# Experts' products on scaled pairs of 16-bit floats, with the weights prepared in the down blocks

## The chip, the cores and the metric

The kernel runs on one core of one Trainium2 chip. The metric is the device time of one execution in microseconds (us); the time before is the median of three runs. A core has TensorE (matrix products, results in PSUM), VectorE, ScalarE and GpSimd (elementwise work; GpSimd has no way into PSUM), and SyncE, whose queue issues the transfers here. In the rows these are PE (its weight loads PEld), DVE, ACT, POOL and SP. Each engine takes its own instructions in the order in which the program issues them, and engines wait for each other through semaphores that the planner of the tiles sets.

## The reference

Attention with a learned position bias, a layer of three gated products, and a layer of eight experts that are mixed by a normalised matrix:

```python
x = attention(q, k, v, bias)                      # 1152 tokens x 512
h = np.maximum(np.maximum(x @ w1, x @ w2), x @ w3)   # 1152 x 768
x = h @ w_out                                     # 1152 x 512
logits = x @ w_gate                               # 1152 x 8
P = np.exp(logits - logits.max())
for _ in range(8):
    P /= P.sum(1, keepdims=True) + 1e-09
    P /= P.sum(0, keepdims=True) + 1e-09
    P *= N / E
for e in range(8):
    out += P[:, e:e+1] * (np.maximum(x @ w1[e], 0) @ w2[e])   # 512 -> 1024 -> 512
```

All inputs are 32-bit floats; moe_w1 to moe_w3 and w_out reach the chip as 64-bit floats.

## The kernel before

Products that need more than the matrix engine's short format are done on pairs: a number is split into a high part (rounded to the short 32-bit format, F32R) and a low part (what is left), and three products, high by high, high by low and low by high, are summed in PSUM. ScalarE rounds the high part, VectorE or GpSimd subtracts for the low part.

The stages in order of time: the bias table (to 74 us), attention (to some 215 us), the first product of the gated layer (`m1_mm`, to 324 us), its output product (L890 to L900, to 362 us), the experts (from 362 us on).

*First product.* 18 pieces, f in 0 to 5 (128 hidden columns) by g in 0 to 2 (384 tokens). Each has three products of 12 matmuls with 384 columns; ScalarE copies the first (`t1`, L784), VectorE takes the two maxima (L786, L789), ScalarE rounds (L790), and VectorE subtracts for the low part one piece later (the list `lows`, L791). Between them `w_step` hands out the preparation of the next weights in single steps: the seven lambdas of `prep_w64` (L105 to L114) on ScalarE, four times VectorE, ScalarE, GpSimd. The order in the program is the order in each engine's queue.

*Output product.* 16 pieces (d by g) of 18 matmuls with 288 columns. ScalarE copies each into `x2f`. The list `steps` puts the work for the experts between the pieces: `x_split` makes high and low parts of the seven blocks that the scheme below needs (`b_steps`, `x_steps`), and `prep_f(0)` the first expert weights.

*Experts.* Each expert has two halves (256 hidden rows of each of two blocks); a half expert h is two "up" blocks, `up(2h)` and `up(2h+1)`, and one "down" block, `down(h)`. The order of issue is up 0, up 1, up 2, down 0, up 3, up 4, down 1, and so on. An up block does a 2x2 block product with seven products in place of eight, each 12 matmuls of 288 columns (two halves of tokens, two slices of the inner dimension, three pairs), into the PSUM tiles x, y and z (two banks each); ScalarE copies partial products out (`snap`), VectorE adds and subtracts, ScalarE rounds the rectified result (`relu_hi`) and VectorE makes the low part (`relu_lo`). A down block has nine tiles of 128 tokens; each is 12 matmuls of 512 columns into one of two banks (`pd`), added to `acc` on VectorE with the weight P. Down 0 and 1 differ: in down 0 ScalarE copies and VectorE does the steps `rows` and `cols` that normalise P, one of eight after each tile, with a small product on TensorE; in down 1 GpSimd multiplies by P.

The weights of an up block come as four blocks (512 KB, `load_f`); `prep_f` makes four sums on VectorE (`s13`, `s24`), rounds on ScalarE (`a_split`, `hi_s`) and subtracts on GpSimd (`a_split`) and VectorE (`lo_s`). The weights of a down block are four tiles of 256 KB (`load_2`, `prep_2`). Both are handed out between the seven products of the up block before (the dictionary `extra`, by the number of the product). `logits` is done on the split parts of x, between products of up 0 (`between`).

## Time and profile before

| what | value |
|---|---|
| three runs | 1127.1, 1127.91, 1130.8 us; median 1127.91 |
| profiled execution | span 1128.2 us (its time is given by its span alone) |
| TensorE busy | 1093.3 us (97%) |
| VectorE, ScalarE, GpSimd busy | 692.3, 497.7, 366.5 us |
| mean granted clock of TensorE | 0.992 |

A profile is one execution. Busy time is the union of an engine's instructions; matmuls overlap in it, so a group's mean is longer than the distance from one matmul to the next. The chain of waits is followed back from the last instruction: at each step to what released it.

### The profile page before, as it was taken

How to read it: one execution, taken by the hardware profiler on the slowest of the kernel's cores; microseconds unless marked ns; L12 is line 12 of the kernel's file. 1: busy time of each engine (PE TensorE's matmuls, PEld its weight loads, DVE VectorE, ACT ScalarE, POOL GpSimd, SP SyncE). 2: the span in 40 equal slices, each digit the busy share in tenths (PEclk: the TensorE clock that was granted, in tenths of full speed). 3: DMA queues.
4: the chain of work that ended last, by engine and by line, in shares of the span. 5: the costliest groups of instructions: out<-in, count | busy, mean ns of one | idle time of the engine just before them, and what ended most of it. 6: DMA issues, size and time to landing. Idle time of an engine off the chain costs nothing.

```text
span 1128.2 us, 18182 instructions
## 1 busy us (share of the span) xinstructions
PE 1093.3 (97%) x7162; PEld 985.8 (87%) x7162; DVE 692.3 (61%) x1214; ACT 497.7 (44%) x903; POOL 366.5 (32%) x258
## 2 busy tenths in 40 slices
...
GB/s 186 266 243 253 217 188 109 40 114 113 109 20 39 76 19 48 28 75 15 62 47 29 76 11 65 48 28 75 13 63 47 28 76 14 62 48 28 57 19 85
DMA packets 36148, 88.49 MB, mean 78 GB/s; under 512 B 5535, under 2 KB 6494, under 8 KB 35166
## 3 DMA queue, kind: packets, MB, share of 16 engines
...
## 4 chain that ended last, share of the span: by engine, by line
PE 76%; DVE 13%; issue 3%; ACT 3%; POOL 2%; DMA 2%; DVEq 0%; SPq 0%; ACTq 0%; POOLq 0%
PE d L1092 35%; PE x L1010 12%; PE y L1010 9%; PE z L1010 8%; PE o L895 3%; PE sc L469 2%; POOL s L343 2%; PE pv L607 2%; DVE ww L106 2%; PE pt L555 1%; DVE ww L111 1%; PE m L658 1%; DVE ng L486 1%; DVE ww L109 1%; PE p L368 1%
## 5 line engine op out<-in xcount | busy, mean ns | idle before, releaser
L1078 POOL TENSOR_TENSOR w2l<-w2r,w2h 128x512 fp32r<-128x512 f32 x64 | 93.6, 1463 | 477.7 <-ACT w2h L1077 469.4
L1106 DVE SCALAR_TENSOR_TENSOR acc<-d,P,acc 128x512 f32<-128x512 f32 x126 | 94.6, 751 | 224.0 <-PE d L1092 223.9
L1092 PE MATMUL d<-w2h,hh 128*128 128x512 f32 x576 | 224.9, 390 | 0.0
L1092 PE MATMUL d<-w2h,hl 128*128 128x512 f32 x576 | 224.6, 390 | 0.0
L1092 PE MATMUL d<-w2l,hh 128*128 128x512 f32 x576 | 224.4, 390 | 0.0
L1018 ACT ACTIVATE s<-x 128x576 f32<-128x576 f32 x96 | 62.5, 651 | 352.8 <-PE x L1010 349.4
L1023 ACT ACTIVATE hh<-s 128x576 fp32r<-128x576 f32 x128 | 87.9, 687 | 93.6 <-DVE s L1035 44.6
L1092 PEld LDWEIGHTS d<-w2h,hl 128*128 128x128 f32 x576 | 108.1, 188 | 23.0 <-DVE hl L1028 0.3
L1092 PEld LDWEIGHTS d<-w2l,hh 128*128 128x128 f32 x576 | 108.2, 188 | 22.0
L1092 PEld LDWEIGHTS d<-w2h,hh 128*128 128x128 f32 x576 | 108.2, 188 | 21.8
L1028 DVE SCALAR_TENSOR_TENSOR hl<-s,hh 128x576 fp32r<-128x576 f32 x128 | 102.1, 815 | 1.8 <-ACT hh L1023 1.5
L835 POOL TENSOR_TENSOR w1l<-wf,w1h 128x768 fp32r<-128x768 f32 x32 | 59.8, 1870 | 77.5 <-ACT w1h L834 67.5
L1010 PE MATMUL x<-xth,w1h 128*128 128x288 f32 x384 | 82.4, 296 | 0.5 <-ACT acc L898 0.5
L1010 PE MATMUL x<-xtl,w1h 128*128 128x288 f32 x384 | 82.2, 296 | 0.0
L1010 PE MATMUL x<-xth,w1l 128*128 128x288 f32 x384 | 82.1, 295 | 0.0
L658 PE MATMUL m<-xh,wh 128*128 128x384 f32 x216 | 73.2, 339 | 2.0 <-DVE t L786 1.9
L658 PE MATMUL m<-xh,wl 128*128 128x384 f32 x216 | 72.8, 337 | 0.7 <-POOL wl L114 0.7
L658 PE MATMUL m<-xl,wh 128*128 128x384 f32 x216 | 72.6, 336 | 0.0
L1044 DVE TENSOR_TENSOR s<-y,s 128x576 f32<-128x576 f32 x32 | 24.2, 757 | 70.4 <-ACT w1h L838 59.4
L1010 PEld LDWEIGHTS x<-xth,w1h 128*128 128x128 f32 x384 | 62.5, 189 | 1.8 <-ACT acc L898 0.7
L1010 PEld LDWEIGHTS x<-xtl,w1h 128*128 128x128 f32 x384 | 61.8, 189 | 0.0
L1010 PEld LDWEIGHTS x<-xth,w1l 128*128 128x128 f32 x384 | 61.8, 189 | 0.0
...
## 6 DMA issues: line engine op xcount, KB each, us to landing
...
w2r<-in_moe_w SPq DMA_DIRECT2D x64, 256.0 KB, 2.6
...
```

What stands on the lines that cost most here:

```text
L106: lambda: V.tensor_scalar(out=f, in0=f, scalar1=2.0 ** -15, scalar2=None, op0=ALU.max),
L658: T.matmul(out=p[:, :TG], lhsT=ws[:, 128 * c:128 * c + 128], rhs=xs[:, c, TG * g:TG * g + TG], start=(c == 0 and n == 0), stop=(c == 3 and ...
L835: G.tensor_tensor(out=lo[:, 0:3], in0=t[:, 1:4], in1=raw(hi[:, 0:3]), op=ALU.subtract)
L895: T.matmul(out=p[:, :SH], lhsT=ws[:, 128 * d:128 * d + 128], rhs=xs[:, f, SH * g:SH * g + SH], start=(k == 0), stop=(k == 17))
L1010: T.matmul(out=ps[bank][:, s, :SH], lhsT=ws[:, i, c, :], rhs=xs[:, j, c, s * SH:s * SH + SH], start=(start and k == 0), stop=(k == 5), **kw)
L1018: A.activation(out=t, in_=src, func=AF.Copy)
L1023: A.activation(out=o, in_=src, func=AF.Relu)
L1028: V.scalar_tensor_tensor(out=l, in0=src, scalar=0.0, in1=raw(o), op0=ALU.max, op1=ALU.subtract)
L1044: V.tensor_tensor(out=s2, in0=y, in1=s2, op=ALU.add)
L1078: G.tensor_tensor(out=lo, in0=r, in1=raw(hi), op=ALU.subtract)
L1092: T.matmul(out=pd, lhsT=hs[:, fh, 128 * t:128 * t + 128], rhs=ws, start=(k == 0), stop=(k == 11))
L1106: V.scalar_tensor_tensor(out=acc[:, t, :], in0=pd, scalar=P[:, t, e:e + 1], in1=acc[:, t, :], op0=ALU.mult, op1=ALU.add)
```

## The change

The operands of the experts' products become pairs of 16-bit floats (F16) in place of pairs in F32R. To keep the numbers in the range of that format, they are multiplied by powers of two: x by one common factor, each half expert's two weight matrices by a factor each, the hidden result by one common factor, and the sum in `acc` is multiplied back (`gains`, `kh`).

- The factors come from largest absolute values. VectorE takes maxima (`peak`): over each piece of the first product's result and over the output weights, over each piece of `x2f`, and over each weight matrix of the experts (`peak_w`). The maxima of the partitions are brought together on TensorE for x and the hidden result (`x_top`, `x_scale`, `m_top`, `m_spread`), and for the expert weights by a transfer to DRAM and one back to all partitions (`peak_send`, `peak_get`), after which VectorE takes the maximum and makes the powers (`peak_all`, `powers`).
- ScalarE multiplies while it copies (a scale per partition): `snap`, the copy of `x2f`, and two new operations, `scale` for a set of up weights and one per tile of down weights, in place.
- The subtraction in `lo_s` goes from VectorE to GpSimd. Adding and subtracting a product in an up block becomes a multiply-add (`join`).
- The preparation of all weights of the experts goes from the up blocks into the down block of the half expert before (the dictionary `todo`, by tile), apart from the first ones. The raw weights are loaded further ahead (four sets of up weights, eight tiles of down weights), and the split down weights have two buffers (`w2s`).
- `logits` uses `x2f` and the gate weights as full 32-bit floats: 16 products with the outputs in four column groups, in place of 40 on split parts.
- In up 0 the first copy is issued after the second product.

```diff
+    peak = [] if top_to is None else [
+        lambda: V.tensor_reduce(out=top_to, in_=f, op=ALU.max, axis=AX.XY, apply_absolute_value=True)]
...
+def powers(out, m):
+
+    i = out.bitcast(I32)
+    n = m.shape[-1]
+    V.tensor_scalar(out=m, in0=m, scalar1=TINY, scalar2=None, op0=ALU.max)
+    V.tensor_scalar(out=i[:, 0:n], in0=m.bitcast(I32), scalar1=EXPM, scalar2=EXPM,
+                    op0=ALU.bitwise_and, op1=ALU.bitwise_xor)
+    V.tensor_scalar(out=i[:, n:2 * n], in0=m.bitcast(I32), scalar1=EXPM, scalar2=None, op0=ALU.bitwise_and)
...
+def peak_out(n, m):
+    w = m.shape[-1]
+    peaks_d[n] = dram.tile([128 * w], F32, name="peaks" + "".join(map(str, n)))
+    dma(peaks_d[n].rearrange("(p w) -> p w", w=w), m)
...
+        w = src.shape[0]
+        peaks_s[n] = scl.tile([128, 256], F32, tag="all", name="all", bufs=2)[:, 0:w]
+        dma(peaks_s[n], src.unsqueeze(0).to_broadcast([128, w]))
...
+def peak_in(n, out):
+    peak_get(n)
+    V.tensor_reduce(out=out, in_=peaks_s.pop(n).rearrange("p (k w) -> p w k", k=128), op=ALU.max, axis=AX.X)
+
+def peak(out, in_):
+    V.tensor_reduce(out=out, in_=in_, op=ALU.max, axis=AX.X, apply_absolute_value=True)
+
+def load_f(n):
+    if n < NE * 4:
+        w1r[n] = (w1e if n % 4 < 2 else w_pool[2]).tile([128, 4, 2, 128], F32, tag="wr1", name="wr1", bufs=2)
+        dma(w1r[n], a["moe2_w1"][n // 4, n % 4])
...
+def peak_all(name, items):
+
+    items = [x for x in items if x[0] < 2 * NE]
+    if items:
+        m = scl.tile([128, 2], F32, tag="pm", name="pm", bufs=2)[:, 0:len(items)]
+        peak_in(name, m)
+        for i, (h, kind) in enumerate(items):
+            o = scl.tile([128, 4], F32, tag=f"pw{kind}", name="pw", bufs=4)
+            powers(o, m[:, i:i + 1])
+            V.tensor_scalar(out=o[:, 2:3], in0=o[:, 0:1], scalar1=2.0 ** (11 if kind == 1 else 13),
+                            scalar2=None, op0=ALU.mult)
+            w_pow[h, kind] = o
...
-        w_pool[:] = mp, 6
+        w_pool[:] = mp, 6, None
+        for n in range(2):
+            load_f(n)
+        S10 = ("a",), [(0, 1)]
+        SB = ("b",), [(1, 1), (0, 2)]
+        SC = ("c",), [(1, 2)]
+        w_early = {(2, 0): lambda: peak_w(0, 1, 0), (2, 2): lambda: [peak_w(0, 1, 1), peak_join(*S10)],
+                   (3, 2): lambda: peak_send(S10[0]), (4, 1): lambda: peak_get(S10[0]),
+                   (5, 1): lambda: peak_all(*S10)}
...
-                lows.append(lambda t2=t2, o=o, l=hl[:, f, TG * g:TG * g + TG]: V.tensor_tensor(
-                    out=l, in0=t2, in1=raw(o), op=ALU.subtract))
+
+                def low(t2=t2, o=o, l=hl[:, f, TG * g:TG * g + TG], m=mo[0][:, 3 * f + g:3 * f + g + 1]):
+                    V.tensor_tensor(out=l, in0=t2, in1=raw(o), op=ALU.subtract)
+                    peak(m, t2)
+
+                lows.append(low)
+                w_early.get((f, g), lambda: None)()
                 w_step(4)
...
-    xth = xtp.tile([128, 7, 2, S], F32R, name="xth")
-    xtl = xtp.tile([128, 7, 2, S], F32R, name="xtl")
...
+    xth = xtp.tile([128, 7, 2, S], F16, name="xth")
+    xtl = xtp.tile([128, 7, 2, S], F16, name="xtl")
...
             return []
-        t = w1f_t.pop(n)
-        hi = w1s.tile([128, 7, 2, 128], F32R, tag="w1h", name="w1h")
-        lo = w1s.tile([128, 7, 2, 128], F32R, tag="w1l", name="w1l")
+        t = w1s.tile([128, 8, 2, 128], F32, tag="wf", name="wf", bufs=1)
+        hi = w1s.tile([128, 7, 2, 128], F16, tag="w1h", name="w1h")
+        lo = w1s.tile([128, 7, 2, 128], F16, tag="w1l", name="w1l")
         w1s_t[n] = hi, lo
+
+        def scale():
+            A.activation(out=t[:, 0:4], in_=w1r.pop(n), func=AF.Identity, scale=w_pow[n // 2, 1][:, 2:3])
+            load_f(n + 4)
...
             A.activation(out=hi[:, 0:3], in_=t[:, 1:4], func=AF.Copy)
-            G.tensor_tensor(out=lo[:, 0:3], in0=t[:, 1:4], in1=raw(hi[:, 0:3]), op=ALU.subtract)
+            G.tensor_tensor(out=lo[:, 0:3], in0=t[:, 1:4], in1=hi[:, 0:3], op=ALU.subtract)
...
         def lo_s():
-            V.tensor_tensor(out=lo[:, 3:7], in0=t[:, 4:8], in1=raw(hi[:, 3:7]), op=ALU.subtract)
-            load_f(n + 1)
-
-        return [s13, s24, a_split, hi_s, lo_s]
+            G.tensor_tensor(out=lo[:, 3:7], in0=t[:, 4:8], in1=hi[:, 3:7], op=ALU.subtract)
+
+        return [scale, s13, s24, a_split, hi_s, lo_s]
...
+    def x_top():
+        pm = ps_s.tile([128, 2, 512], F32, tag="sc", name="pmh")
+        T.transpose(pm[:2, 0, :128], mho, ident)
+        V.tensor_reduce(out=nho, in_=pm[:2, 0, :128], op=ALU.max, axis=AX.X)
+        V.tensor_scalar(out=dho, in0=ident[0:2, 0:2], scalar1=nho, scalar2=None, op0=ALU.mult)
...
+    def x_scale():
+        pm = ps_s.tile([128, 2, 512], F32, tag="sc", name="pmh2")
+        T.matmul(out=pm[:, 0, 0:2], lhsT=ones[0:2, :], rhs=dho, start=True, stop=True)
+        V.tensor_copy(out=mho, in_=pm[:, 0, 0:2])
+        powers(pho, mho)
+        for i in range(2):
+            V.tensor_scalar(out=xs[:, i:i + 1], in0=pho[:, 2 * i:2 * i + 1], scalar1=pho[:, 2 * i + 1:2 * i + 2],
+                            scalar2=0.5, op0=ALU.mult, op1=ALU.mult)
...
+    bs0, bs1, xs0, pf0, last = b_steps(0), b_steps(1), x_steps(0), prep_f(0), []
+    pf1 = prep_f(1)
+    sched = {0: [x_top], 1: [x_scale], 2: [pf0[0]], 3: [pf0[1], pk(1, 1, 0)], 4: [pf0[2], pk(1, 1, 1), bs0[0]],
+             5: [pf0[3], pk(0, 2, 0), bs0[1]], 6: [pf0[4], pk(0, 2, 1), pk(0, 2, 2)],
+             7: [pk(0, 2, 3), lambda: peak_join(*SB), pf0[5]],
+             8: xs0[0:2], 9: xs0[2:4], 10: xs0[4:5] + pf1[0:1] + [lambda: peak_send(SB[0])], 11: pf1[1:3],
+             12: bs1[0:1] + pf1[3:4], 13: bs1[1:2] + pf1[4:5] + [lambda: peak_get(SB[0])],
+             14: [lambda: last[0]()], 15: [lambda: last[1](), pf1[5]]}
...
+            def x_ev(k=k, p=p, o=x2f[:, d, SH * g:SH * g + SH]):
+                A.activation(out=o, in_=p[:, :SH], func=AF.Identity, scale=xs[:, 0:1])
+                peak(xm[:, k:k + 1], o)
+
+            evs.append(x_ev)
+            if k < 2:
+                sched[k][0]()
+            if k > 0:
+                while evs:
+                    evs.pop(0)()
+            if k == 15:
+                V.tensor_reduce(out=m2[:, 0:1], in_=xm, op=ALU.max, axis=AX.X)
+            for step in sched.get(k, ())[k < 2:]:
                 step()
...

-    def logits(b):
-
-        blocks = ((0, 0), (1, 1)) if b == 0 else ((0, 0), (0, 3), (1, 2))
-        for n in range(2):
-            p = ps_d.tile([128, 512], F32, tag="d", name="pl")
-            mm = [(ws, xs[:, blk, c, n * SH:n * SH + SH], 2 * dh + c)
-                  for dh, blk in blocks for c in range(2) for ws, xs in zip(wgs, (xth, xtl))]
-            for k, (ws, xs, c) in enumerate(mm):
-                T.matmul(out=p[0:2 * NE, :SH], lhsT=ws[:, c, :], rhs=xs, start=(k == 0), stop=(k == len(mm) - 1))
-            A.activation(out=lt[:, b * S + n * SH:b * S + n * SH + SH], in_=p[0:2 * NE, :SH], func=AF.Copy)
+    def logits():
+
+        p = ps_d.tile([128, 512], F32, tag="d", name="pl")
+        for k in range(4):
+            for c in range(4):
+                T.matmul(out=p[32 * c:32 * c + NE, :SH], lhsT=wg[:, k, :], rhs=x2f[:, k, SH * c:SH * c + SH],
+                         start=(k == 0), stop=(k == 3))
+        for c in range(4):
+            A.activation(out=lt[:, SH * c:SH * c + SH], in_=p[32 * c:32 * c + NE, :SH], func=AF.Identity,
+                         scale=xs[0:NE, 1:2])
...
+    def m_top():
+        pm = ps_d.tile([128, 512], F32, tag="d", name="pmx")
+        T.transpose(pm[:1, :128], m2[:, 0:1], ident)
+        V.tensor_reduce(out=nm2, in_=pm[:1, :128], op=ALU.max, axis=AX.X)
+
+    def m_spread():
+        pm2 = ps_d.tile([128, 512], F32, tag="d", name="pmx2")
+        T.matmul(out=pm2[:, 0:1], lhsT=ones[:1, :], rhs=nm2, start=True, stop=True)
+        V.tensor_copy(out=m2[:, 1:2], in_=pm2[:, 0:1])
+        powers(cx[:, 0:2], m2[:, 1:2])
+        V.tensor_scalar(out=c, in0=cx[:, 0:1], scalar1=2.0 ** -9, scalar2=None, op0=ALU.mult)
+        V.tensor_scalar(out=nc_, in0=c, scalar1=-1.0, scalar2=None, op0=ALU.mult)
+        V.tensor_scalar(out=kx, in0=cx[:, 1:2], scalar1=xs[:, 1:2], scalar2=2.0 ** 8, op0=ALU.mult, op1=ALU.mult)
+
+    between = {(0, 0): [m_top, last[2]], (0, 1): [m_spread, last[3]], (0, 3): [last[4], logits], (1, 0): [flip], (1, 1): [gate],
+               (0, 4): [lambda: peak_all(*SB)], (0, 6): [pk(1, 2, 0), pk(1, 2, 1)], (1, 5): [],
+               (1, 2): [pk(1, 2, 2), pk(1, 2, 3), lambda: peak_join(*SC)],
+               (1, 4): [lambda: peak_send(SC[0])], (2, 2): [lambda: peak_get(SC[0])], (2, 5): [lambda: peak_all(*SC)]}
...
+    def gains(h):
+        kh = kh_t[h] = sk.tile([128, 1 + NTT], F32, tag="kh", name="kh", bufs=2)
+        o1, o2 = w_pow[h, 1], w_pow[h, 2]
+        V.tensor_scalar(out=kh[:, 0:1], in0=o1[:, 1:2], scalar1=o2[:, 1:2], scalar2=kx, op0=ALU.mult, op1=ALU.mult)
+        V.tensor_scalar(out=kh[:, 0:1], in0=kh[:, 0:1], scalar1=2.0 ** -26, scalar2=None, op0=ALU.mult)
+        if h > 1:
+            V.tensor_scalar(out=kh[:, 1:], in0=P[:, :, h // 2], scalar1=kh[:, 0:1], scalar2=None, op0=ALU.mult)
...
-        hhi = h_p.tile([128, 2, NT], F32R, tag="hh", name="hh")
-        hlo = h_p.tile([128, 2, NT], F32R, tag="hl", name="hl")
+        hhi = h_p.tile([128, 2, NT], F16, tag="hh", name="hh")
+        hlo = h_p.tile([128, 2, NT], F16, tag="hl", name="hl")
...
-            A.activation(out=t, in_=src, func=AF.Copy)
+            A.activation(out=t, in_=src, func=AF.Identity, scale=c)
             return t
+
+        def join(out, z, scale):
+            V.scalar_tensor_tensor(out=out, in0=z, scalar=scale, in1=out, op0=ALU.mult, op1=ALU.add)
...
-        s1 = snap("s1", prod(A11, B11, "x", True))
+        x = prod(A11, B11, "x", True)
+        if n > 0:
+            s1 = snap("s1", x)
         then(0)
         z = prod(A12, B21, "z", True)
-        V.tensor_tensor(out=s1, in0=z, in1=s1, op=ALU.add)
+        if n == 0:
+            then(1)
+            s1 = snap("s1", x)
+        join(s1, z, c)
         relu_hi(0, 0, s1)
-        then(1)
+        if n > 0:
...
         y = prod(S4, B22, "y", False)
-        V.tensor_tensor(out=s2, in0=y, in1=s2, op=ALU.add)
...
-        V.tensor_tensor(out=s3, in0=s3, in1=z, op=ALU.subtract)
+        join(s3, z, nc_)
...
             c, fh = i // 2 % 2, i % 2
-            hi = w2p.tile([128, DM], F32R, tag=f"w2h{c}{fh}", name="w2h")
-            lo = w2p.tile([128, DM], F32R, tag=f"w2l{c}{fh}", name="w2l")
+            hi = w2s.tile([128, DM], F16, tag=f"w2h{c}{fh}", name="w2h")
+            lo = w2s.tile([128, DM], F16, tag=f"w2l{c}{fh}", name="w2l")
             r = w2r.pop(i)
+            A.activation(out=r, in_=r, func=AF.Identity, scale=w_pow[i // 4, 2][:, 2:3])
             A.activation(out=hi, in_=r, func=AF.Copy)
-            G.tensor_tensor(out=lo, in0=r, in1=raw(hi), op=ALU.subtract)
-            w2t[c, fh] = hi, lo
-            load_2(i + 2)
+            G.tensor_tensor(out=lo, in0=r, in1=hi, op=ALU.subtract)
+            w2t[i // 4, c, fh] = hi, lo
+            load_2(i + 8)
...
+        kh = kh_t.pop(h)
+        S2 = (h,), [(h + 2, 1), (h + 2, 2)]
+        p2 = lambda i: lambda: prep_2(4 * (h + 1) + i)
+        fa, fb = ((prep_f(n) or [lambda: None] * 6) for n in (2 * h + 3, 2 * h + 4))
+        todo = {0: [fa[0], pk(h + 2, 1, 0), pk(h + 2, 1, 1)], 1: [fa[1], pk(h + 2, 2, 0), pk(h + 2, 2, 1)],
+                2: [fa[2], pk(h + 2, 2, 2), pk(h + 2, 2, 3), lambda: peak_join(*S2), lambda: peak_send(S2[0])],
+                3: [fa[3], lambda: peak_get(S2[0])], 4: [fa[4], fa[5]], 5: [p2(0), lambda: peak_all(*S2)],
+                6: [fb[0], fb[1], p2(1)], 7: [fb[2], fb[3], p2(2)], 8: [p2(3), fb[4], fb[5]]}
...
-                A.activation(out=acc[:, t, :], in_=pd, func=AF.Copy)
+                A.activation(out=acc[:, t, :], in_=pd, func=AF.Identity, scale=kh[:, 0:1])
...
-                V.tensor_tensor(out=acc[:, t, :], in0=pd, in1=acc[:, t, :], op=ALU.add)
+                V.scalar_tensor_tensor(out=acc[:, t, :], in0=pd, scalar=kh[:, 0:1], in1=acc[:, t, :],
+                                       op0=ALU.mult, op1=ALU.add)
                 pool_scale(acc[:, t, :], acc[:, t, :], P[:, t, 0:1])
             else:
-                V.scalar_tensor_tensor(out=acc[:, t, :], in0=pd, scalar=P[:, t, e:e + 1], in1=acc[:, t, :],
+                V.scalar_tensor_tensor(out=acc[:, t, :], in0=pd, scalar=kh[:, 1 + t:2 + t], in1=acc[:, t, :],
                                        op0=ALU.mult, op1=ALU.add)
+            for f in todo[t]:
+                f()
...
-            extra = {i: [f] for i, f in enumerate(prep_f(n + 1))}
-
-            for seg in ((0, 1, 3, 5) if n in (0, 4 * NE - 1) else (0, 5)):
-                if n not in (1, 2):
-                    extra.setdefault(seg, []).append(lambda i=piece: prep_2(i))
-                    piece += 1
+            extra = {}
+            if n == 1:
+                extra = {i: [f] for i, f in enumerate(prep_f(2))}
+            for seg, i in {0: ((5, 0),), 1: ((1, 1), (4, 2)), 2: ((1, 3),)}.get(n, ()):
+                extra.setdefault(seg, []).append(lambda i=i: prep_2(i))
+            if n and (n % 2 == 0 or n == 4 * NE - 1):
+                extra.setdefault(3, []).append(lambda n=n: gains(n // 2 - (n % 2 == 0)))
```

## Rows read from the trace of the kernel before

**Rows 1.** The page's first part: busy time, share of the span, instructions.
```profile
PE 1093.3 (97%) x7162; PEld 985.8 (87%) x7162; DVE 692.3 (61%) x1214; ACT 497.7 (44%) x903; POOL 366.5 (32%) x258
```
**Rows 2.** Stretches: from:to, length, busy (instructions) of PE PEld DVE ACT POOL; PEclk.
```profile
228.00:324.00 96.00, 93.46 (x531) 91.44 (x530) 72.26 (x122) 35.15 (x68) 24.65 (x19) 1.00 0.31 94
...
900.00:946.90 46.90, 46.90 (x278) 42.64 (x277) 24.12 (x35) 16.14 (x24) 9.61 (x6) 1.00 0.16 46
```
**Rows 3.** Chain that ended last, a half expert: start, length in us, what.
```profile
875.78 24.53 PE d L1092 x108
...
922.70 24.53 PE d L1092 x108
```
**Rows 4.** Timeline of TensorE, warm-up, cut after two and after five matmuls.
```profile
4.42 0.86 PE L232 MATMUL p<-wz 128*128 128x512 bf16 x2
...
4.42 1.50 PE L232 MATMUL p<-wz 128*128 128x512 bf16 x5
```
**Rows 5.** Timeline of TensorE, bias stage, cut after four and after sixteen matmuls.
```profile
58.48 0.39 PE L368 MATMUL p<-s,wb 128*32 128x498 f16 x4 [0.51 <-POOL s L343]
...
58.48 1.02 PE L368 MATMUL p<-s,wb 128*32 128x498 f16 x16 [0.51 <-POOL s L343]
```
**Rows 6.** Chain that ended last: the logits, and a step's sum over tokens.
```profile
369.21 2.11 PE pl L938 x16
...
374.50 3.16 PE pl L938 x24
...
408.80 0.17 PE pc L977 x2
```
**Rows 7.** Groups by line and shape: busy us, mean ns | idle before and its releaser.
```profile
L841 DVE TENSOR_TENSOR w1l<-wf,w1h 128x1024 fp32r<-128x1024 f32 x32 | 39.3, 1229 | 1.1 <-ACT w1h L838 1.1
...
L978 DVE TENSOR_REDUCE col<-pc 128x8 f32<-128x72 f32 x8 | 1.9, 233 | 9.7 <-PE pc L977 9.7
...
L979 DVE TENSOR_SCALAR col<-col 128x8 f32<-128x8 f32 x8 | 1.4, 171 | 0.3
...
L1023 ACT ACTIVATE hh<-s 128x576 fp32r<-128x576 f32 x128 | 87.9, 687 | 93.6 <-DVE s L1035 44.6 <-DVE s L1044 26.1 <-DVE s L1049 17.5
...
L497 ACT ACTIVATE pe<-ng,st 128x576 f32<-128x576 f32 x72 | 55.8, 774 | 4.2 <-DVE st L486 4.0
...
L838 ACT ACTIVATE w1h<-wf 128x1024 fp32r<-128x1024 f32 x32 | 33.7, 1054 | 2.3 <-DVE wf L831 2.3
...
L1078 POOL TENSOR_TENSOR w2l<-w2r,w2h 128x512 fp32r<-128x512 f32 x64 | 93.6, 1463 | 477.7 <-ACT w2h L1077 469.4 <-DVE wf L826 8.3
L835 POOL TENSOR_TENSOR w1l<-wf,w1h 128x768 fp32r<-128x768 f32 x32 | 59.8, 1870 | 77.5 <-ACT w1h L834 67.5 <-PE x L1010 10.0
```
**Rows 8.** Chain, weight tiles of the gated layer: where it leaves VectorE between two.
```profile
248.09 0.52 issue
248.61 0.65 ACT ww L105
```
**Rows 9.** Timeline of VectorE, first down block: first and last of eight dependent steps.
```profile
409.01 0.23 DVE L978 TENSOR_REDUCE col<-pc 128x8 f32<-128x72 f32 x1 [2.32 <-PE pc L977]
...
410.71 0.23 DVE L973 TENSOR_TENSOR P<-P,row 128x72 f32<-128x72 f32 x1
```
**Rows 10.** DMA issues: size of one, median us to landing.
```profile
r<-r_d SPq DMA_DIRECT2D x7, 256.0 KB, 4.0
```
**Rows 11.** Timeline of VectorE: one subtraction with GpSimd at work and without.
```profile
353.74 1.54 DVE L831 TENSOR_TENSOR wf<-wf 128x256 f32<-128x256 f32 x1
...
904.86 0.43 DVE L831 TENSOR_TENSOR wf<-wf 128x256 f32<-128x256 f32 x1
```
**Rows 12.** Groups by line and shape on GpSimd: 16-bit and 32-bit elements.
```profile
L343 POOL TENSOR_SCALAR s<-rs,thr 128x564 f16<-128x564 f16 x3 | 5.1, 1699 | 9.9 <-DVE thr L239 9.9
L64 POOL TENSOR_SCALAR xh<-x 128x576 fp32r<-128x576 f32 x6 | 4.0, 675 | 0.5
```

129 lines of the change are left out of this document (81 added, 48 removed).

## Prediction

> **What bounds the kernel now.** I read first the page's busy line, then stretches of the span, then the chain that ended last, then single instructions. TensorE is busy 97% of the span of 1128.2 us [rows 1]. By itself that says little, so the stretches follow: in the steady experts a whole half expert takes 46.9 us and TensorE is busy for all of it, VectorE 24.1, ScalarE 16.1, GpSimd 9.6 us [rows 2]. The chain of waits agrees: it is nothing but matmuls there, a "down" block of 108 matmuls in 24.53 us, and the next such block starts 46.92 us after the last one [rows 3]. What lies between, 46.92 - 24.53 = 22.39 us, is two "up" blocks of 84 matmuls each. So in this stage no engine but TensorE matters, and only the distance from one matmul to the next does: 24.53 / 108 = 227.1 ns at 512 columns and 22.39 / 168 = 133.3 ns at 288 columns, where one column per cycle of 2.4 GHz (the granted clock is 1.00 in these rows) would be 213.3 and 120.0 ns. Every one of these matmuls carries 11 to 14 ns more. Ahead of the experts it is different: in the first product of the gated layer, at 228 to 324 us, TensorE is busy 93.5 of 96 us and VectorE 72.3 us [rows 2].
>
> **Does the excess belong to the 32-bit operands?** Only few matmuls of the trace have 16-bit operands. The warm-up does 128x512 in bf16, each with its own weight load: three further ones lengthen the run from 0.86 to 1.50 us, that is 213 ns each, at most 217 with the rounding of the rows [rows 4]. The bias stage has 16-bit floats in four column groups side by side: twelve more of 498 columns, three rounds, take 1.02 - 0.39 = 0.63 us, 210 ns a round against 207.5 ns of columns [rows 5]. So both 16-bit forms cost their columns and 2 to 3 ns. I take 216 ns for 512 columns and, with the same 2.5 ns, 122.5 ns for 288 columns. The second has no row of its own; its bounds are 120 (columns alone) and 133.3 (no gain).
>
> **The terms.**
> 1. Down: 16 half experts x 108 = 1728 matmuls, 227.1 to 216 ns: -19.2 us (-20 to 0).
> 2. Up: 32 x 84 = 2688 matmuls, 133.3 to 122.5 ns: -29.0 us (-36 to 0).
> 3. Logits: 40 matmuls in 2.11 + 3.16 = 5.27 us go [rows 6]. In their place come 16 full 32-bit ones, each of which is two instructions: the 72-column ones of `cols` take 0.17 us a pair [rows 6], so 288 columns are 4 x 0.12 = 0.5 us at least, 16 of them 8 us in a row, but they lie in four column groups, which [rows 5] shows running side by side: 2 us. Between +2.7 and -3.3 I take -3, since the column groups have rows.
> 4. First product of the gated layer (228 to 324 us): each of 18 pieces gets a maximum over 384 elements on VectorE, right after its low part. A reduce of 72 elements takes 233 ns, a subtraction of 1024 takes 1229 [rows 7], so about 0.55 us for one of 384, 0.47 beyond the overlap with its neighbour. Two maxima of 1024 (1.2 us each) for the first expert's weights join them, and six of 512 for the output weights. VectorE has the time on average (72 + 15 of 96 us), but the chain runs through it all along this stretch: the preparation of the weights goes VectorE, ScalarE, VectorE, and TensorE waits now and then for the maximum L786, which is queued behind. VectorE waits about 1.2 us per weight tile for ScalarE [rows 8]; the six of 512 fall into that gap, and a third of the rest. 13 pieces x 0.47 x 0.7 + 2.4 = 6.7 us on VectorE's chain, of which TensorE's two banks of lead take some: +4 us. Bounds 0 and +13.
> 5. Entry of the experts: the common scale of x is known only when the last piece of the output product is copied out and its maximum taken (0.45 + 0.45 us for 288 elements, by the slopes of [rows 7]); it passes TensorE twice and seven small VectorE operations of 0.17 us [rows 7], behind x_steps' subtractions. Up 0 defers its first copy by one product (1.5 us), which covers most of it. In up 1 VectorE and ScalarE have about 10.5 us of work each in a block of 10.3. +3 us (0 to 6).
> 6. The first down block: its chain of normalising steps is eight dependent VectorE operations, from 409.01 to 410.94, some 2 us [rows 9] per tile of about 2.9 us (24.53 / 9 and a pair of `pc` matmuls). The change puts 2.0 to 2.6 us of maxima and sums behind them in tiles 0 to 2 and the scales in tile 5; the next `cols` matmul on TensorE waits for the row step. By adding up tile by tile, the waits are 0.8, 1.7 and 1.1 us: +3.5 us (0 to 6).
> 7. Steady half experts, per 43.9 us. VectorE: 24.1, less two subtractions of 1.23, plus two maxima of 1.2, four of 0.7, two joins 0.5, one `peak_all` 2.0, `gains` 0.6: 30 us. ScalarE: 16.1 plus two scalings of 1.1 and four of 0.7, and 0.09 on eight copies (a pointer operand: 774 against some 690 ns [rows 7]): 22 us. GpSimd: 9.6 plus two subtractions of 1024, 2.3 us each by the slope of [rows 7]: 14.2 us. All have room. What each waits for: in down, `fa` starts at tile 0, its VectorE sums follow tile 2's addition (9.5 us in), its high part is ready at 10.6 and its low part at about 13 of 23.3 us. The DRAM round trip of the maxima is issued after tile 2 (10 us) and two transfers of about 4 us (a broadcast from DRAM lands in 4.0 us [rows 10]) end at 18; VectorE reaches `peak_all` behind tile 5's addition at 16.5 and may stand there 2 us; tile 6's addition behind it then starts 1 to 2 us late, and TensorE needs that bank only at 20.7. On SP nothing urgent stands behind the two transfers. ScalarE's last piece of `fb` at tile 8 ends about when the next up's first copy is due, and TensorE needs that copy three products later. +1 us in all (0 to 8).
>
> On item 7 there is a rule against the change. First the row: the subtraction L831 of 256 elements took 1.54 us while GpSimd was subtracting and 0.43 us otherwise [rows 11]. The Trainium skill ("GPSIMD Engine Reference", Specifications and Engine selection) says that GpSimd shares its SBUF interface with VectorE and contends with VectorE instructions of two SBUF inputs, and would leave elementwise work on VectorE. This trace agrees on the contention.
>
> In numbers of the rows: VectorE has about 10 us of operations with two SBUF inputs per half expert and GpSimd is busy a third of the time, so VectorE grows by a third of 10 x 2.6, to 39 us, still under 43.9. If all of them met GpSimd, VectorE would reach 56 us and be the bound.
>
> **Sum.** -19.2 - 29.0 - 3 + 4 + 3 + 3.5 + 1 = -39.7 us on a span of 1128.2: 1088.5. The runs' median, 1127.9, lies 0.3 us from that span, so the time is 1088 us.
>
> **Rivals.**
> A. *GpSimd takes longer on 16-bit parts, slower than before.* For: on GpSimd a compare of 564 16-bit elements takes 1699 ns and a product of 576 32-bit elements 675 ns [rows 12], 2.6 times as long per element. Against: the operations differ, and no 16-bit subtraction is in the trace. Place: the single `wf` buffer and GpSimd's order in the down block, lo_s, two w2l, w1l, two w2l, lo_s, from 10.8 us on: 2.3 + 2.9 + 1.9 + 2.9 + 2.3 = 12.3 us, wanted by the third product of the second up at 23.3 + 10.3 + 2.9 = 36.5. So it decides from 25.7 / 12.3 = 2.1 times on. At 2.6 times it is 6 us late in each of 14 half experts: 1088 + 84 = 1172 us.
> B. *The 16-bit parts don't shorten the matmuls* (the excess comes from changing weights and not from the operand width): terms 1 and 2 vanish, the added ones stay: 1136 us. Against: both 16-bit rows change or reload weights. For: none of them has 128x128 weights that differ each time.
> C. *The lead-in costs more*: items 4 to 7 at their upper ends (13 + 6 + 6 + 8 instead of 11.5): 1110 us. For: the chain through VectorE ahead of 311 us.
> D. *Matmuls overlap further and TensorE stops being the bound.* Then VectorE's 30 to 39 us per half expert, say 36, would be: 1128 - 16 x (46.9 - 36) + 8 for the lead-in (items 3 to 7) = 962 us. Against: the 213 ns of [rows 4] are from back-to-back matmuls and are the columns at one per cycle. The Trainium skill ("TensorE: Matmul & The Clock Gate", Back-to-back issue gap) gives for a sustained stream of load-and-multiply pairs 131 ns at 512 columns and 81 at 128, which would be this case. The rows here don't bear it out.
>
> **How the numbers follow.** Forecast 0.82; A 0.06; B 0.04; C 0.07; D 0.01. Range: from all added terms at zero (1128 - 52 = 1076) up into C, whose cases lie between 1096 and 1112: 1076 to 1106 leaves out A, B, D and a part of C, with some of the forecast's own tail. A measurement of this kernel can tell about 0.3% (3.4 us) from no change. Faster: forecast, C, D: 0.90. Slower: A and most of B: 0.08. Within: 0.02.
>
> **What would show it.** Down blocks of 108 matmuls in 23.3 us and half experts 43.9 us apart show terms 1 and 2; 24.5 and 46.9 show B. A chain that passes GpSimd's w1l between a down block and the third product of the second up shows A. Gaps of TensorE at 228 to 324 us ahead of L786's successor show item 4, gaps ahead of the `pc` matmuls in the first down block item 6. If half experts come at 43.9 us and the time still is above 1106, the lead-in is mispriced.

## The result, and the profile after

| | before | after |
|---|---|---|
| median of the runs | 1128.98 us (1127.1 to 1130.8, 4 runs) | 1098.8 us (1096.58 to 1099.89, 4 runs) |
| ratio, 95% interval | | 0.9731 (0.9714 to 0.9748) |
| profiled execution, its span | 1128.2 us span | 1099.56 us, 1097.8 us span |

The change makes the kernel 30 us faster; 40 were forecast (1088, range 1076 to 1106). The steady experts first. The page's busy line, and below it the same stretch as in [rows 2], one half expert, now 43.90 us long (from:to, length, busy us and instructions of PE, PEld, DVE, ACT, POOL, then the granted clock):

```profile
PE 1049.3 (96%) x7160; PEld 737.1 (67%) x7160; DVE 799.5 (73%) x1559; ACT 587.4 (54%) x999; POOL 407.9 (37%) x286
```
```profile
620.94:664.84 43.90, 43.90 (x278) 27.03 (x277) 30.34 (x54) 21.96 (x32) 12.93 (x10) 1.00 0.21 54
```

TensorE is busy throughout, VectorE 30.3, ScalarE 22.0 and GpSimd 12.9 us of it: forecast were 30, 22 and 14.2. The chain that ended last answers to [rows 3] (start, length, what):

```profile
620.89 0.22 PE d L1276
621.10 1.47 PE x L1186 x12
622.57 1.47 PE z L1186 x12
...
641.68 23.31 PE d L1276 x108
```

23.31 / 108 = 215.8 ns at 512 columns and 1.47 / 12 = 122.5 ns at 288: the two figures that the forecast took (216 and 122.5). Now the lead-in, in five stretches: first gated product up to its last stage; that last stage (`o`); up blocks 0 to 2; down block 0 up to up block 3; up blocks 3 and 4.

```profile
198.26:326.56 128.30, 124.18 (x698) 120.75 (x697) 102.30 (x186) 45.69 (x88) 28.39 (x22) 0.99 0.33 91
326.56:365.76 39.20, 38.94 (x293) 38.48 (x292) 24.94 (x51) 18.41 (x31) 12.50 (x9) 1.00 0.32 108
365.76:411.31 45.55, 38.25 (x301) 27.57 (x300) 32.39 (x63) 27.98 (x44) 15.10 (x10) 0.93 0.19 40
411.31:443.51 32.20, 26.37 (x126) 12.13 (x124) 28.89 (x94) 16.99 (x24) 9.20 (x7) 1.00 0.21 53
443.51:465.76 22.25, 22.25 (x170) 17.13 (x170) 11.93 (x20) 10.46 (x15) 3.13 (x2) 0.92 0.08 25
```

The same stretches of the kernel before are 123.54, 38.83, 40.59, 26.58 and 22.85 us long, all at a granted clock of 1.00. So the lead-in, where the shorter matmuls should also have saved some 9 us, grew by 15.1 us, and three of its stretches have a granted clock below 1: in a part of each TensorE ran at 1.2 instead of 2.4 GHz (below, "the half clock"), in or behind waits. What it waits for at the experts' entry is in the chain:

```profile
364.12 1.06 ACT w1h L948
365.18 0.40 ACT acc L1041
...
366.05 1.42 DVE ta L967
367.47 0.02 issue
367.49 0.69 ACT xth L957
368.18 0.02 issue
368.20 1.85 DVE xtl L958
370.05 0.37 DVE xm L807
```
```profile
PE pmx L1138 <- DVE m L1051: 3.4, 1, 3.4
```

The second fence is the view of waits: the transpose of the maximum (L1138) stands 3.4 us. The maximum of the last piece (`xm`, L807) comes behind two subtractions of the last combinations, and these behind a rounding of the second up block's weights (`w1h`, L948). After it the 12 matmuls of `z` take 2.88 us instead of 1.47. In down block 0 the waits ahead of the column sums (`pc`, L1122) are 5.7 us together. The timeline of VectorE there, and below it GpSimd's in the same stretch:

```profile
428.10 0.23 DVE L1123 TENSOR_REDUCE col<-pc 128x8 f32<-128x72 f32 x1 [0.60 <-PE pc L1122]
428.37 1.98 DVE L1124 TENSOR_SCALAR col<-col 128x8 f32<-128x8 f32 x1
430.38 0.20 DVE L1125 RECIPROCAL col<-col 128x8 f32<-128x8 f32 x1
430.62 0.23 DVE L1126 SCALAR_TENSOR_TENSOR P<-P,col 128x72 f32<-128x72 f32 x1
```
```profile
428.20 2.12 POOL L951 TENSOR_TENSOR w1l<-wf,w1h 128x1024 f16<-128x1024 f32 x1 [2.22 <-ACT w1h L948]
```

Adding a constant to 128 x 8 elements, 0.17 us in [rows 7], takes 1.98 us: it starts while GpSimd subtracts and ends within 0.03 us of GpSimd's end (430.35 to 430.32). Before, GpSimd was idle in this block.

### The profile page after: what moved, and what is told of

Same layout as the page of the kernel before. It is cut to its first block, busy times and chain, and to the rows that moved or that the text cites. A ratio compares the mean times of both kernels' runs of the same rounds, so it can differ in the third digit from the quotient of the medians.

```text
span 1097.8 us, 18483 instructions
## 1 busy us (share of the span) xinstructions
PE 1049.3 (96%) x7160; PEld 737.1 (67%) x7160; DVE 799.5 (73%) x1559; ACT 587.4 (54%) x999; POOL 407.9 (37%) x286
## 4 chain that ended last, share of the span: by engine, by line
PE 72%; DVE 17%; ACT 4%; issue 3%; POOL 2%; DMA 1%; DVEq 0%; ACTq 0%; SPq 0%; POOLq 0%
PE d L1276 32%; PE x L1186 12%; PE y L1186 8%; PE z L1186 8%; PE sc L476 3%; PE pv L614 2%; PE pt L562 2%; PE m L665 2%; PE o L1037 2%; POOL s L350 1%; DVE ww L117 1%; DVE ww L112 1%; DVE ww L115 1%; DVE ng L493 1%; DVE ptl L576 1%
## 5 line engine op out<-in xcount | busy, mean ns | idle before, releaser
L1276 PE MATMUL d<-w2h,hl 128*128 128x512 f16 x576 | 218.3, 379 | 0.2 <-DVE hl L1207 0.2
L1276 PE MATMUL d<-w2h,hh 128*128 128x512 f16 x576 | 218.3, 379 | 0.0
L1276 PE MATMUL d<-w2l,hh 128*128 128x512 f16 x576 | 218.3, 379 | 0.0
L1186 PEld LDWEIGHTS <-w1h 128*128 128x128 f16 x1792 | 175.9, 98 | 53.1 <-issue 5.2
L1276 PEld LDWEIGHTS <-hh 128*128 128x128 f16 x1152 | 112.8, 98 | 131.5 <-issue 0.4
L1202 ACT ACTIVATE hh<-s 128x576 f16<-128x576 f32 x128 | 87.4, 683 | 127.1 <-DVE s L1198 101.6
L945 POOL TENSOR_TENSOR w1l<-wf,w1h 128x768 f16<-128x768 f32 x32 | 55.2, 1724 | 257.0 <-ACT w1h L944 239.2
L1207 DVE SCALAR_TENSOR_TENSOR hl<-s,hh 128x576 f16<-128x576 f32 x128 | 109.5, 857 | 49.1 <-ACT hh L1202 46.4
L1291 DVE SCALAR_TENSOR_TENSOR acc<-d,kh,acc 128x512 f32<-128x512 f32 x126 | 94.0, 746 | 67.3 <-PE d L1276 66.8
L1254 POOL TENSOR_TENSOR w2l<-w2r,w2h 128x512 f16<-128x512 f32 x64 | 77.1, 1214 | 117.3 <-ACT w2h L1253 117.3
L1186 PEld LDWEIGHTS <-w1l 128*128 128x128 f16 x896 | 88.3, 99 | 22.9
L948 ACT ACTIVATE w1h<-wf 128x1024 f16<-128x1024 f32 x32 | 33.6, 1050 | 84.5 <-DVE wf L941 84.5
L1186 PE MATMUL x<-xth,w1l 128*128 128x288 f16 x384 | 78.7, 287 | 0.0
```

The source lines that it names most:

```text
L945: G.tensor_tensor(out=lo[:, 0:3], in0=t[:, 1:4], in1=hi[:, 0:3], op=ALU.subtract)
L1186: T.matmul(out=ps[bank][:, s, :SH], lhsT=ws[:, i, c, :], rhs=xs[:, j, c, s * SH:s * SH + SH], start=(start and k == 0), stop=(k == 5), **kw)
L1202: A.activation(out=o, in_=src, func=AF.Relu)
L1207: V.scalar_tensor_tensor(out=l, in0=src, scalar=0.0, in1=o, op0=ALU.max, op1=ALU.subtract)
L1254: G.tensor_tensor(out=lo, in0=r, in1=hi, op=ALU.subtract)
L1276: T.matmul(out=pd, lhsT=hs[:, fh, 128 * t:128 * t + 128], rhs=ws, start=(k == 0), stop=(k == 11))
```

## The experiments

Stage lengths in us, as in the five stretches above; "rest" is from there to the last matmul's start; in brackets what the half clock adds to matmuls of that stretch, summed over their steps. Medians in the last column (before: 1128 to 1129 in every comparison). Each row's stretches are from one profiled run, and a stretch that an edit leaves alone differs between runs too: "rest" is 627.9 us in the changed kernel, and 630.0 to 631.6 us in the seven kernels from `maximum_first` to `no_peaks`, whose edits all end ahead of it. So the median is a weak measure of an edit worth 1 or 2 us, and the stretch that was edited is read first.

| kernel | product | o | up 0-2 | down 0 | up 3-4 | rest | median |
|---|---|---|---|---|---|---|---|
| before | 123.5 | 38.8 | 40.6 | 26.6 | 22.9 | 671.3 | 1129.0 |
| after | 128.3 (1.6) | 39.2 | 45.6 (2.0) | 32.2 | 22.3 (1.6) | 627.9 | 1098.8 |
| types_alone | 123.5 | 38.8 | 38.6 | 24.7 | 21.4 | 630.8 | 1086.7 |
| fixed_factor | 129.3 (3.4) | 39.2 | 45.7 (1.9) | 32.1 | 22.3 (1.7) | 630.5 | 1102.6 |
| maximum_first | 126.8 | 39.2 | 46.8 (1.6) | 32.2 | 20.6 | 630.0 | 1104.4 |
| second_later | 128.8 | 39.2 | 46.0 (1.7) | 32.2 | 20.6 | 630.2 | 1103.1 |
| earlier | 127.3 (1.6) | 39.2 | 44.2 | 32.2 | 20.6 | 630.1 | 1098.9 |
| slots | 128.9 (3.1) | 39.2 | 43.4 | 32.2 | 20.6 | 631.6 | 1098.7 |
| rounds_later | 128.7 (1.4) | 39.2 | 44.8 | 30.3 | 22.9 (1.6) | 631.5 | 1100.6 |
| gpsimd_later | 128.0 (1.6) | 39.2 | 44.8 (1.4) | 29.4 | 21.1 | 631.6 | 1097.9 |
| no_peaks | 128.6 (1.6) | 38.8 | 44.8 (1.1) | 32.2 | 22.3 (1.6) | 631.5 | 1104.4 |
| together | 126.7 | 39.2 | 42.0 | 29.4 | 21.1 | 633.7 | 1099.0 |
| gpsimd_added | 124.1 (1.6) | 38.8 | 40.6 | 32.6 | 22.5 | 671.5 | 1134.9 |
| types_further | 122.3 | 36.0 | 38.6 | 24.7 | 20.6 | 634.7 | 1082.0 |

**The operand type alone** (on the kernel before).

```diff
-                xth = xtp.tile([128, 7, 2, S], F32R, name="xth")
+                xth = xtp.tile([128, 7, 2, S], F16, name="xth")
...
-                        hi = w2p.tile([128, DM], F32R, tag=f"w2h{c}{fh}", name="w2h")
+                        hi = w2p.tile([128, DM], F16, tag=f"w2h{c}{fh}", name="w2h")
```

> The kernel before with nothing changed but the element type of the experts' operands (and of the gate's): F32R becomes F16 in xth, xtl, w1h, w1l, the hidden parts, w2h, w2l and wgs; no scales, no peaks, no moved preparation. Theory W (the width of the operands sets the spacing of the matmuls): 108 matmuls of 512 columns in each of 16 down blocks at 215.8 ns for 227.1 and 2688 of 288 columns at 122.5 ns for 133.3 take off 19.5 + 29.0 us: 1129 - 48.5 = about 1080 us (1077 to 1085), a down block 23.3 us and a product 1.47 us, and nothing of the lead-in's waits. Rival M (it is the move of the weights' preparation out of the up blocks that lets the matmuls run): the spacing falls, but the up blocks stay near 22 us, waiting for VectorE and ScalarE, and with the down blocks' gain alone it ends at 1100 to 1111 us. Rival B (the parts' width does nothing, the change's gain is from elsewhere): 1127 to 1131 us.

Measured: 1086.68 us (1083.83 to 1087.68), ratio 0.9623 (0.9602 to 0.9644). One half expert:

```profile
600.00:643.90 43.90, 43.90 (x278) 27.01 (x277) 23.73 (x35) 15.71 (x24) 8.93 (x6) 1.00 0.16 49
```

The same 43.90 us as in the changed kernel, with VectorE at 23.7 instead of 30.3 us: the step between matmuls comes from the operands' type (F16 for F32R) and nothing else of the change. The span is 46 us shorter than before, the median 41; in the profile three up blocks wait some 1 us for a copy. M and B fall; W has the step right, and its time (1077 to 1085) is missed by 1.7 us. And the rest of the change (scales, peaks, moved preparation) costs 1098.8 - 1086.7 = 12 us.

**The entry: is it the round trip of the maximum?**

```diff
+                c, nc_ = 2.0 ** -12, -2.0 ** -12
                 def m_top():
-                    pm = ps_d.tile([128, 512], F32, tag="d", name="pmx")
...
+                    pass
```

> The changed kernel with the factor of the accumulators' copies written as the constant 2^-12 in place of the one worked out from the maximum of the first expert's input: the transpose, the reduction, the spreading matmul and the powers at the experts' entry are left out, as is that part of the computation. Theory R (the round trip of the maximum is what the entry waits for, and the half clock after it is its consequence): the wait of 3.5 us before the transpose goes, with it the two products at the half clock (some 2.4 us) and the two small matmuls with their waits (some 0.8 us): 1098.8 - 6.7 = about 1092 us (1090.5 to 1094), and TensorE's granted clock stays at 1.0 from 360 to 400 us. Rival Q (VectorE and ScalarE are behind with the last eighth of the input's combinations, the third product needs them anyway): the wait moves to the third product and to the copies of the up blocks 0 to 2, and 0 to 3 us are gained: 1096 to 1099 us.

Measured: 1102.6 us (1100.95 to 1103.69), above the ranges of both theories. Up blocks 0 to 2 take 45.7 us as before the edit. TensorE's waits there:

```profile
PE x L1180 <- ACT s L1188: 4.5, 1, 4.5
PE y L1180 <- DVE xtl L958: 0.9, 1, 0.9
```

The 3.4 us come back two products later, with the half clock behind them. R falls. Of Q the place is right, not the time: what is late is the work that the third and fourth product need. In the profiled run the 4 us more than in the changed kernel lie in the first product (1.0) and in "rest" (2.6), which the entry's wait does not reach; their cause is not shown.

```diff
-                         14: [lambda: last[0]()], 15: [lambda: last[1](), pf1[5]]}
+                         15: [pf1[5], lambda: last[0]()]}
...
-                between = {(0, 0): [m_top, last[2]], (0, 1): [m_spread, last[3]], (0, 3): [last[4], logits], (1, 0): [flip], (1, 1): [gate],
+                between = {(0, 0): [m_top, last[1], last[2]], (0, 1): [m_spread, last[3]], (0, 3): [last[4], logits], (1, 0): [flip], (1, 1): [gate],
```

> The changed kernel with the first two steps of the last combinations of the expert's input moved behind the last tile's copy, its peak and the reduction of all peaks; the second one goes into the first up block. Theory R in its form for the queue (the maximum waits because VectorE and ScalarE, in order, hold those two steps ahead of it): the reduction ends about 3 us sooner, the wait of 3.5 us before the transpose falls to 1 us or less, the third product waits up to 1.5 us for its operand, and the half clock goes or is shorter: 1098.8 less 3 to 5.5 = 1093 to 1096 us. Rival Q: the wait only moves to the third product and the clock falls there: 1097 to 1100 us.

Measured: 1104.35 us (1101.15 to 1106.71). The transpose no longer waits, but the matmul that spreads the maximum does (2.3 us, for VectorE), and the fourth product 3.0 us. Q's place again, and again above its range (1097 to 1100).

```diff
-                         8: xs0[0:2], 9: xs0[2:4], 10: xs0[4:5] + pf1[0:1] + [lambda: peak_send(SB[0])], 11: pf1[1:3],
-                         12: bs1[0:1] + pf1[3:4], 13: bs1[1:2] + pf1[4:5] + [lambda: peak_get(SB[0])],
-                         14: [lambda: last[0]()], 15: [lambda: last[1](), pf1[5]]}
+                         8: xs0[0:2], 9: xs0[2:4], 10: xs0[4:5] + [lambda: peak_send(SB[0])], 11: pf1[0:1],
+                         12: bs1[0:1], 13: bs1[1:2] + [lambda: peak_get(SB[0]), lambda: last[0]()],
+                         15: [lambda: last[1]()]}
...
+                        if n == 0:
+                            extra = {i: [f] for i, f in enumerate(pf1[1:])}
```

> The changed kernel with the preparation of the second up block's weights (all but its scaling) moved from the end of the first gated product's last stage into up block 0, where the kernel before has it, and with the first step of the input's last combinations one tile earlier; nothing is left out. Theory K (at the end of that stage this second preparation holds VectorE, GpSimd and ScalarE, so that the last combinations and the maximum behind them come late; the two experiments at the entry only moved the wait within that queue): the wait of 3.5 us at the entry falls to 1 us or less without coming back at the third and fourth product, and the half clock of 2 us goes: 1093.5 to 1096 us. Rival Q (the work is the same, the wait comes back in up block 0, where the preparation now stands among the copies): 1097 to 1102 us.

Measured: 1103.05 us (1101.79 to 1106.18). The wait before the transpose is gone, but in up block 0 stand 0.5, 2.9 and 1.8 us for VectorE's and ScalarE's copies; 46.0 us in all. That is Q's place, 1 us above its range.

```diff
-                         8: xs0[0:2], 9: xs0[2:4], 10: xs0[4:5] + pf1[0:1] + [lambda: peak_send(SB[0])], 11: pf1[1:3],
-                         12: bs1[0:1] + pf1[3:4], 13: bs1[1:2] + pf1[4:5] + [lambda: peak_get(SB[0])],
-                         14: [lambda: last[0]()], 15: [lambda: last[1](), pf1[5]]}
+                         8: xs0[0:2], 9: xs0[2:4] + pf1[1:2], 10: xs0[4:5] + bs1[0:1] + pf1[2:3] + [lambda: peak_send(SB[0])],
+                         11: bs1[1:2] + pf1[3:4], 12: pf1[4:6], 13: [lambda: peak_get(SB[0]), lambda: last[0]()],
+                         15: [lambda: last[1]()]}
```

> The changed kernel with the second up block's weights prepared earlier in the first gated product's last stage (additions in the tiles 9 and 10 for 11, both subtractions of GpSimd over two tiles sooner) and the first step of the last combinations in tile 13 for 14; nothing is left out, nothing goes into the up blocks. Theory E (at the entry VectorE's last combinations and the maximum are late because that preparation comes last, its GpSimd subtractions of 1.8 and 2.6 us and the additions they hold up standing right ahead of them; taken up or down the queue by themselves, as in the three kernels before, the combinations stay behind it): the reduction of all peaks ends less than 1 us after the stage's last matmul, the waits of 3.5 us before the transpose and of 0.7 and 1.2 us behind it fall to 1 us together, the half clock goes: 1098.8 - 4 to 6.5 = 1092 to 1095 us. Rival Q (that stage's end has more work on VectorE than time, wherever it stands): 1097 to 1101 us.

Measured: 1098.91 us (1098.22 to 1101.71). The wait before the transpose shrinks to 2.7 us only. `rounds_later`, whose up blocks 0 to 2 are unedited and ran at the full clock, has 44.8 us there; this one 44.2. E gets 0.6 us of the 4 to 6.5 it expected.

**Up blocks 1 and 2.**

```diff
-                            extra = {i: [f] for i, f in enumerate(prep_f(2))}
-                        for seg, i in {0: ((5, 0),), 1: ((1, 1), (4, 2)), 2: ((1, 3),)}.get(n, ()):
+                            extra = {i: [f] for i, f in zip((0, 1, 2, 3, 5, 5.5), prep_f(2))}
+                            extra[5] = extra[5] + extra.pop(5.5)
+                        for seg, i in {0: ((5, 0),), 2: ((0, 1), (3, 2), (5, 3))}.get(n, ()):
```

> The changed kernel with three preparations of second weights and one rounding of first weights in the up blocks 1 and 2 put behind the copies of the first and the fourth product and behind the last copy, where ScalarE waits for the joins anyway, and no longer just ahead of a copy; nothing is left out. Theory S (the four waits of 1.26, 1.35, 0.68 and 1.27 us in these blocks are ScalarE's two instructions for a second weight, 1.25 us, standing ahead of a copy that frees a PSUM bank): they fall to under 1 us together: 1098.8 - 3.9 = about 1095 us (1094 to 1096.5). Rival A (ScalarE or VectorE has too much work in these blocks whatever the order): 1097.5 to 1100 us.

Measured: 1098.72 us (1097.94 to 1099.62). The stretch takes 43.4 us, 1.3 less than in `rounds_later` at the same clock. What is left has other causes:

```profile
PE pm L1107 <- DVE nm L1103: 1.0, 1, 1.0
PE y L1186 <- ACT s L1194: 0.7, 1, 0.7
PE y L1186 <- POOL w1l L951: 0.6, 1, 0.6
```

S is right for a third of these waits (1.3 of 3.9 us), and the median stays where the rival A has it (1097.5 to 1100).

**Down block 0.**

```diff
-                            if t > 0:
+                            if t > 2:
                                 cols()
-                            if t < 8:
+                            if t > 1:
                                 rows()
...
+                           (3, 1): [lambda: cols(1), rows], (3, 4): [lambda: cols(1)]}
```

> The changed kernel with the gate's eight rounds of normalisation begun two tiles later in the first down block, behind the peaks of half expert 2, so that the last two rounds' column sums fall into up block 3; nothing is left out. Theory D (the column sums of the first down block wait because their VectorE steps stand behind those peaks, and the half clock in up block 3 comes from the last of these waits): of the 6.9 us of waits ahead of the column sums 4 to 5 go, and the 1.7 us of the half clock with them, while two column sums in up block 3 cost some 0.4 us: 1093 to 1095 us. Rival V (VectorE has no room in that block whatever the order): the waits move to the later tiles and into up block 3, and it stays at 1097.5 to 1100 us.

Measured: 1100.57 us (1098.85 to 1103.58). The block is 1.9 us shorter, not 4 to 5, and two column sums in up block 3 take 0.6 back; the time is 0.6 above the range of V. Moving VectorE's own queue isn't enough. Then the other side, GpSimd alone, on the kernel before:

```diff
                             if t < 8:
                                 rows()
+                            if 0 < t < 8:
+                                for _ in range(2):
+                                    G.tensor_tensor(out=dl, in0=acc[:, t, :], in1=dl, op=ALU.subtract)
```

> The kernel before (F32R, no scales) with work added on GpSimd alone: in tiles 1 to 7 of the first down block two subtractions of 128 x 512 into a scratch tile that nobody reads, behind the tile's copy out of PSUM; VectorE, ScalarE and TensorE get no instruction more. Theory G (a VectorE addition, multiplication or comparison that starts while GpSimd works ends only with GpSimd's instruction; in the changed kernel's first down block those of the normalisation do so behind the preparation's subtractions): each tile's normalisation, which just fits into a tile's matmuls, is held up by 1 to 2 us, TensorE waits for it ahead of the column sums, and the block grows from 26.6 us by 7 to 14: 1135 to 1143 us. Rival V (the waits of the changed kernel's first down block are VectorE's own added work, and GpSimd's is free): 1127 to 1131 us.

Measured: 1134.91 us (1134.27 to 1135.57), ratio 1.0049 (1.0033 to 1.0064). The block grows from 26.6 to 32.6 us. VectorE's timeline in one tile, and GpSimd's:

```profile
413.20 0.43 DVE L981 TENSOR_SCALAR col<-col 128x8 f32<-128x8 f32 x1
413.66 0.20 DVE L982 RECIPROCAL col<-col 128x8 f32<-128x8 f32 x1
413.89 1.04 DVE L983 SCALAR_TENSOR_TENSOR P<-P,col 128x72 f32<-128x72 f32 x1
414.97 0.23 DVE L972 TENSOR_REDUCE row<-P 128x9 f32<-128x72 f32 x1
```
```profile
412.43 2.41 POOL L1106 TENSOR_TENSOR dl<-acc,dl 128x512 f16<-128x512 f32 x2 [0.65 <-ACT acc L1099]
```

VectorE has no instruction more and still comes late: the addition (0.17 us elsewhere) ends with GpSimd's first subtraction, 413.63 to 413.60, and the product (0.23 us elsewhere) with its second, 414.93 to 414.84; the reciprocal between them is not held. V falls. The size, +6 us, is just under the 7 to 14 of G. Taking GpSimd's work out of the changed kernel's block is the counterpart:

```diff
+                    if h == 0:
+                        todo.update({5: [lambda: peak_all(*S2)], 6: [], 7: [], 8: []})
+                        later.update({(3, s): [f] for s, f in zip((0, 1, 2, 3, 5), fb)})
+                        later[3, 5].append(fb[5])
+                        later.update({k: [p2(i)] for i, k in enumerate(((3, 6), (4, 0), (4, 3), (4, 5)))})
```

> The changed kernel with one preparation of first weights and the four of second weights taken out of the second half of the first down block and put into the up blocks 3 and 4, as the kernel before has them; nothing is left out. Theory G (the later three waits ahead of column sums, 0.28, 0.33 and 2.12 us, are VectorE's instructions held up by GpSimd's subtractions there): they go, and the half clock in up block 3 with them (1.6 us): 1098.8 - 4.3 = about 1094.5 us, up to 1096 with what the subtractions then hold up in the up blocks. Rival V: only four additions leave VectorE's queue there, 1.7 us of the last wait at most: 1097 to 1100 us.

Measured: 1097.89 us (1096.26 to 1099.88). In its place G holds: the block is 2.8 us shorter, the last three waits are gone, up blocks 3 and 4 have the full clock, 3.9 us together for 4.3 expected. But the median moves by 0.9, into the range of V. In the profiled run "rest" is 3.7 us longer: from down block 1 on VectorE stands up to 3.1 us for the returning peaks, long enough that a tile's addition and TensorE behind it wait 0.2 to 1.0 us in seven blocks. The waits of VectorE here and, in the second line, in the changed kernel's profile:

```profile
DVE pm L804 <- DMA all<-peaks: 30.7, 13, 3.1
DVE pm L804 <- DMA all<-peaks: 24.4, 13, 2.2
```

That is not a price of this edit. `slots`, `rounds_later` and `no_peaks` have the same wait (30.0 to 30.6 us in all, 2.9 to 3.1 at most) and 3.6 to 3.7 us more of "rest", and no edit there. What made it shorter in the changed kernel's profiled run is not shown.

**The first gated product.**

```diff
                                 V.tensor_tensor(out=l, in0=t2, in1=raw(o), op=ALU.subtract)
-                                peak(m, t2)
...
-                    V.tensor_reduce(out=mho[:, i:i + 1], in_=mo[0][:, (0, 18)[i]:(18, 24)[i]], op=ALU.max, axis=AX.X)
+                    V.memset(mho[:, i:i + 1], (0.1925, 0.1631)[i])
```

> The changed kernel without the 18 + 6 peaks of the hidden values and of the output weights in the first gated product: the two maxima behind the product's scale are written as constants, and finding them is the part left out. Theory P (14 us of added VectorE work in a stage whose VectorE was already 77% busy is what makes it longer, 128.1 us for 123.4 from its first to its last matmul, with the half clock of 1.5 us that follows its waits): the stage comes back to 123.5 to 124.5 us and the whole to 1094 to 1095 us. Rival L (the stage waits for its weights, which stand in one queue with the experts' first weights, as the wait of 6.65 us for a transfer in the chain has it): it stays above 126.5 us, 1097 to 1100 us.

Measured: 1104.36 us (1103.55 to 1104.99), above the ranges of both theories, the stretch 128.6 us. VectorE is busy 93.6 us in it, 8.7 less, and nothing is gained: P's gain fails to come, and the stretch stays above 126.5 us, as L has it. But the same length is made of other waits. The chain, with one of the first expert's two peaks that were left in (`pk`), and TensorE's largest wait:

```profile
274.63 1.06 DVE ww L112
276.15 1.14 DVE pk L806
277.84 0.70 DVE ww L115
...
296.62 0.69 DVE ww L115
298.44 8.08 DMA wr<-in_moe_w
306.60 0.67 ACT ww L111
```
```profile
PE m L664 <- DVE t L883: 4.5, 4, 2.2
```

One transfer of weights takes 8.08 us; the others of its kind land after 4.0 (median). It is in every kernel with the change (6.5 to 8.7 us, at about 298 us, the first transfer of weights behind the send of the first peaks) and in none of the four without (5.0 at most in `types_alone`, 4.3 or 4.4 in the others). That fits L, but it does not make up the 4.8 us. Matmul by matmul (648 in this stage of each kernel), the changed kernel is 1.5 us behind the kernel before at 304 us, when the slow transfer lands, 3.5 at 310.5, and the rest comes with the half clock from 311 us on: so the transfer is worth some 2 us and perhaps that half clock. `no_peaks` has lost 3.7 of its 5.1 us by 285 us, ahead of the transfer: the wait of 2.2 us ends at 280.9, behind the peak that was left in, and the half clock follows it there; some 2 us come behind the transfer. So neither P nor L is settled. Why the transfer is slow was not tried, nor a kernel without the two peaks of the first expert's weights, some 1.1 us each.

**Three rearrangements at once** (`earlier`, `slots`, `gpsimd_later`, and the returning peaks taken up one tile later).

> The changed kernel with three rearrangements at once: the second weights' preparation earlier, the second weights of the up blocks 0 to 2 behind copies where ScalarE waits anyway, the preparations of the first down block's second half in the up blocks 3 and 4; and in every half expert the reduction of the returned peaks one tile later. Nothing is left out. If the lead-in's waits are the queues' order and GpSimd's hold on VectorE, as the single kernels have it, their gains add: entry 5, up blocks 1 and 2 2.5, first down block and up block 3 4, and no waits for the returning peaks in the down blocks: 1098.8 - 11 = about 1088 us (1085 to 1091). If the work of the lead-in is what it is and the waits only change places: 1095 to 1099 us.

Measured: 1099.04 us (1096.99 to 1100.37). The lead-in does get shorter: up block 5 starts 8.4 us sooner than in the changed kernel (480.74 for 489.15), with the full clock throughout; 1.6 of them are the first product's length, which none of the edits touches, and the three stretches behind it are 7.6 us shorter, of 11 expected. The time is that of the second theory (1095 to 1099), since what follows gives 5.8 us back: with the factors a tile later (no other kernel has that edit) the next up block waits some 0.39 us each time for a copy.

```profile
PE y L1186 <- ACT s L1194: 3.5, 13, 0.6
```

**A version that beats both.**

```diff
-                hh = hp.tile([128, 6, NT], F32R, name="hh")
+                hh = hp.tile([128, 6, NT], F16, name="hh")
...
-                woh = [hp.tile([128, DM], F32R, name=f"woh{f}") for f in range(6)]
+                woh = [hp.tile([128, DM], F16, name=f"woh{f}") for f in range(6)]
```

> The kernel with F16 in place of F32R for the experts' operands and no scales (types_alone), and F16 also for the operands of the first gated product's last stage: the hidden parts hh, hl and the output weights woh, wol. Nothing is left out. Theory W (the step between matmuls goes with the operands' width in any stage): the 288 matmuls of 288 columns of that stage fall from 133.3 to 122.5 ns, 3.1 us, the stage from its first to its last matmul from 38.0 to about 35 us, and the time from 1086.7 to about 1083.6 us (1082 to 1085). Rival Y (at that stage's end VectorE's combinations of the expert's input are late already, as the entry's experiments say of the changed kernel): the matmuls end 3 us sooner and the wait of 0.65 us ahead of the first up block grows by as much: 1086 to 1088 us.

Measured: 1082.01 us (1079.34 to 1082.34, 5 runs), ratio 0.9573 (0.956 to 0.9586): 17 us faster than the changed kernel, 47 than the one before. The `o` stage:

```profile
321.63:357.58 35.95, 35.45 (x289) 28.19 (x289) 13.12 (x17) 14.48 (x29) 11.18 (x8) 1.00 0.11 31
```

35.95 us for 38.83: 2.9 of the 3.1 expected, in another stage, and the wait ahead of the first up block stays at 0.65 us. Y falls. Both of these versions leave out the scales by which the change keeps its numbers in the range of the format; no run here tries inputs of another size.

## Why the prediction was right where it was, and wrong where it wasn't

The sum, item by item, in us; measured from the profiled spans (for a lead-in stretch: its growth plus what the shorter steps should have taken off it).

| item | forecast | measured | from |
|---|---|---|---|
| 1 down | -19.2 | -19.5 | 1728 x (227.1 - 215.8) ns |
| 2 up | -29.0 | -29.0 | 2688 x (133.3 - 122.5) ns |
| 3 logits | -3 | -3.2 | 5.27 to 2.06 |
| 4 first product | +4 | +4.8 | 128.30 - 123.54 |
| 5 entry, up 0-2 | +3 (0 to 6) | +11.3 | 4.96 + 2.7 + 3.2, and 0.4 in `o` |
| 6 down 0 | +3.5 (0 to 6) | +8.0 | 5.62 + 1.2, and 1.2 in up 3-4 |
| 7 steady | +1 | -0.6 | 671.34 - 627.91 against 42.8 of steps |
| not of the change | 0 | -1.9 | the product's start, 200.19 to 198.26 |

The measured column sums to -30.1, the spans differ by 30.4.

The measured 1098.8 us lie in the range, 10.8 above the forecast's 1088. That is the ground of rival C (cases between 1096 and 1112, chance 0.07), and the range held because its upper end had been drawn into C. That the kernel became faster, and the larger part of the sum, came from items 1 to 3, which held; items 5 and 6 failed.

*Items 1 to 3* were right, and for items 1 and 2 `types_alone` shows that the reason was right. The two rows of 16-bit matmuls [rows 4, 5] carried the 2.5 ns over to a form that the trace did not have. Rivals B and D are out; of D, the Trainium skill ("TensorE: Matmul & The Clock Gate", Back-to-back issue gap) has 131 ns at 512 columns, and measured were 215.8. The side-by-side column groups of the logits hold: 2.06 us.

*Rival A* is out (`w2l` and the first part of `w1l` by groups): GpSimd is not slower on 16-bit parts but faster, 1214 ns for 512 elements and 1724 for 768, for 1463 and 1870 in [rows 7].

*Item 4* had the right size, which is luck as far as the runs tell. The sum was built on VectorE's added maxima; without 24 of them the stretch is as long. The chain also holds a slow transfer, worth some 2 us, and the half clock, which the sum did not have; the cause of the 4.8 us stays open.

*Item 5* is the step that failed most. It priced the round trip of the maximum, some seven small operations, and let a deferred copy cover it. `fixed_factor` takes the round trip away and gains nothing: the late ones are the engines that make the third and fourth product's operands. The change had put a second preparation of weights into the `o` stage, and the prediction's part by part does not count what that puts ahead of the last combinations: additions, roundings and two GpSimd subtractions. In that timeline three of VectorE's operations are long (1.40, 1.49 and 1.85 us for 0.42, 0.75 and 0.76) with GpSimd at work, and they end 0.28, 0.62 and 0.62 us behind GpSimd's instruction, as held operations of their sizes do elsewhere in this trace; that GpSimd is the reason at this place was not tried by itself. The cause of item 5 as a whole is argued from where the waits went, not shown: no run takes that work away. Four edits of the entry moved the wait, and each by itself took off at most 0.6 us. In up blocks 1 and 2 "about 10.5 us of work each in a block of 10.3" was seen, but not that a copy that frees a bank stands behind other work.

*Item 6* had the mechanism (column sums wait for VectorE) with only VectorE's own work in it. GpSimd, idle there before, now does seven subtractions of 9.2 us in the block, and seven of VectorE's operations last 6.0 us longer in all than the same shapes elsewhere. Seven column sums come late, by 0.49, 0.86, 1.36, 1.50, 0.28, 0.33 and 2.13 us beyond a step of 0.22. The first three stand where GpSimd has held VectorE for 0.2 us only: 2.7 us, for which the prediction had 3.6. The other four, 4.2 us, stand behind held operations, and `gpsimd_later` takes the last three away. The prediction had the row for it [rows 11] and weighed it, but in item 7 alone, where a half expert has room. There it cost nothing in the changed kernel's profiled run (-0.6); in the seven profiled runs named above, with the same steady blocks, item 7 comes to +1.4 to +3.1 us for the forecast's +1 (0 to 8), by the wait that it named: `peak_all` standing for the returning peaks, 2.2 us at most in the one and 2.7 to 3.1 in the others. In the one block where the chain of small steps just fits into a tile it decides, as `gpsimd_added` shows (+6 us from GpSimd alone). The Trainium skill speaks of an exclusive lock between VectorE and GpSimd, not a shared bandwidth ("Trainium Architecture — The Big Picture", What this means for kernel authors); the timelines agree: held operations end 0.03 to 0.62 us behind GpSimd's.

*Rival C* named this place at 1110 us with each item at its upper bound. Items 5 and 6 went past their bounds, items 4 and 7 stayed under theirs, which made 1098.8. No item had a term for the half clock: 5.2 us in the profiled run.
